# Second layer of two small networks: weight halves side by side in one 512-column matmul, the halves added by ScalarE's copy and GpSimd

## The chip, the core and the metric

The kernel runs on one core of a Trainium2 chip. Its engines are TensorE (PE; PEld is its weight load), VectorE (DVE), ScalarE (ACT), GpSimd (POOL) and the DMA queue of SyncE (SP). TensorE writes to PSUM, a small memory of accumulation banks (512 float32 columns each here); the other tiles lie in SBUF. The metric is the time of one execution in device microseconds. Before the change the median of three runs is 865.88 us (861.5 to 867.78).

## What is computed

The input is 2 x 3136 rows of 256 numbers. A Fourier filter with soft thresholds comes first, then two mixtures (small two-layer networks, each added to its input), the second behind a real two-dimensional Fourier transform:

```python
def _moe_ref(x, g_ln, w_ch1, w_ch2):
    mu = np.mean(x, axis=-1, keepdims=True)
    var = np.mean((x - mu) ** 2, axis=-1, keepdims=True)
    xn = (x - mu) / np.sqrt(var + 1e-06) * g_ln
    ch = np.maximum(xn @ w_ch1, 0.0) @ w_ch2       # 256 -> 1024 -> 256
    return (x + ch).astype(np.float32)

def _moe2_ref(x, w_ch1, w_ch2):
    mixed = np.real(np.fft.fft(np.fft.fft(x, axis=1), axis=2)).astype(np.float32)
    u = x + mixed                                  # then as above, without g_ln
    ...
    return (u + ch).astype(np.float32)
```

## The kernel before, in words

Matmuls run on operands rounded to 12 bits of mantissa (float32r). To keep float32's accuracy each operand is split into a main part and a rest (`h` and `l`), and a product is three matmuls into one PSUM tile: main x main, main x rest, rest x main (`mm3`, `mm3r`).

Rows go through the mixtures in chunks of up to four tiles of 128 rows, 13 chunks for each mixture (26), 49 tiles each. Per chunk (`Chunk`, driven by `run_mlp`): `prep` normalizes the next chunk's rows on VectorE (statistics, then four scalings into `q`), `trans` transposes them on TensorE, `l1(f)` makes one of eight blocks of 128 hidden channels for all rows of the chunk (six matmuls of up to 512 columns into a `psa` tile; ScalarE writes the main part after the relu, VectorE the rest), and `l2(i)` makes the output of one row tile (for each of the eight blocks three matmuls of 256 columns into a `psb` tile, 24 in all), after which VectorE adds the tile's input and `store` sends it out. A `psb` tile is one PSUM bank of 512 columns, of which 256 are used; there are two of them. The stationary operand of the second layer is the hidden block, the moving one the weights.

The weights come as float64, and `decode64` on VectorE splits them into main part and rest, in an SBUF tile `r3a` for the first mixture and `r2b` for the second. Each has a half of main parts and a half of rests; `w_views` names their pieces.

Between the mixtures stands a 98-point transform of each of the two batch halves (`Stage98`), 16 steps for each: load a piece of `dX`, three GpSimd instructions on it (`split`), a ScalarE copy, a subtraction on VectorE or GpSimd (the rest), three matmuls into `psc`, a ScalarE copy out, a small GpSimd copy, a store to `dA`. The first half's 16 steps hang on the chunks 7 to 10 of the first mixture, since they need all of that half's rows, the last of which chunk 6 stores; the second half's hang on chunks 0 to 3 of the second mixture, since they need the first mixture's last chunk. VectorE, ScalarE and GpSimd each take their instructions in the order of the program, which a scheduler lays out with its own estimate of times; an instruction that waits holds up all behind it on its engine.

`wk` tiles rotate over a few buffers by tag. Tag `t98` (TB = 2) has two buffers, used before the change by the inverse transform's tiles alone, which ends before the first chunk's second layer.

## Time and profile before

| | |
|---|---|
| median of three runs | 865.88 us (861.5 to 867.78) |
| the profiled execution: its own time | 860.46 us |
| its span, first to last instruction | 858.7 us |
| TensorE matmul busy | 824.3 us, 96% of the span, 5235 matmuls |
| VectorE, ScalarE, GpSimd busy | 529.8, 282.1, 129.5 us |
| granted TensorE clock | 0.986 of full speed in the mean |

The profile is that of one execution. Busy time of TensorE overlaps, since a matmul is shown until it leaves the pipeline; the distance between starts of matmuls tells what one costs. "Idle before" with an arrow names what ended an engine's wait. The chain of waits is followed back from the last instruction.

### The profile page before, as it was taken

To read this page: it belongs to the slowest core of one execution; us is meant where nothing else is said; L and a number is where in the kernel's file an instruction comes from. 1 tells how busy PE (TensorE), PEld (TensorE's weight loads), DVE (VectorE), ACT (ScalarE), POOL (GpSimd) and SP (SyncE) were. 2 spreads that over 40 slices of the span, in tenths; PEclk is the share of its full clock that TensorE was granted. 3 is DMA by queue.
4 is the path that set the end of the run, shared out by engine and by line. 5 is a ranking of instruction groups with operands and counts; after the bars stand their busy time and mean duration, and the time that the engine had idled before them with its cause. 6 is when DMAs were issued, how large, how long until landed. Compare 5 with 4: busy or idle time off the path is not lost.

```text
span 858.7 us, 13585 instructions
## 1 busy us (share of the span) xinstructions
PE 824.3 (96%) x5235; PEld 719.0 (84%) x5235; DVE 529.8 (62%) x1216; ACT 282.1 (33%) x541; POOL 129.5 (15%) x184
## 2 busy tenths in 40 slices
PE   7999999868999999998999998999999999999997
PEld 2778978824999989986989997888899899999996
DVE  5677999476456894458557356476456656445652
ACT  0222355246222222244342224334432323322321
POOL 0112321220100000069310005244120000000000
PEclk9999999969999999999999999999999999999999
DMA  8630201534110321155223104433323122210001
GB/s 229 182 101 27 74 27 49 175 123 142 59 50 18 108 78 50 63 152 155 79 96 116 61 26 115 119 97 112 117 64 88 46 65 63 74 50 22 17 21 30
DMA packets 47956, 71.66 MB, mean 83 GB/s; under 512 B 11748, under 2 KB 32236, under 8 KB 47696
## 3 DMA queue, kind: packets, MB, share of 16 engines
q1 hardware_dynamic: 47892, 70.80, 27.4%
q8 instruction: 41, 0.67, 0.3%
q14 instruction: 23, 0.19, 0.1%
HBM read 45.09 MB, written 25.69 MB: 82 GB/s over the span
## 4 chain that ended last, share of the span: by engine, by line
PE 80%; DMA 8%; DVE 6%; POOL 2%; SPq 2%; issue 1%; ACT 1%; POOLq 0%; DVEq 0%
PE psb L212 10%; PE psb L210 10%; PE psb L211 10%; PE psa L216 9%; PE psa L217 9%; PE psa L218 9%; PE psb L457 7%; PE psc L323 3%; PE psc L578 2%; PE psc L679 2%; PE psc L477 2%; DMA r<-dX 2%; PE psa L425 2%; PE psc L305 1%; DMA h<-in_x_dram 1%; DMA stg<-in_w_i_dram 1%
## 5 line engine op out<-in xcount | busy, mean ns | idle before, releaser
L602 ACT ACTIVATE h<-psa 128x512 fp32r<-128x512 f32 (+2 forms) x208 | 118.1, 572 | 264.1 <-PE psa L218 252.9
L603 DVE SCALAR_TENSOR_TENSOR h<-psa,h 128x512 fp32r<-128x512 f32 (+2 forms) x208 | 135.0, 653 | 89.6 <-ACT h L602 88.4
L212 PE MATMUL psb<-r3a,h 128*128 128x256 f32 x392 | 108.9, 284 | 2.0 <-DVE h L603 2.0
L210 PE MATMUL psb<-r2b,h 128*128 128x256 f32 x392 | 110.7, 286 | 0.0
L210 PE MATMUL psb<-r3a,h 128*128 128x256 f32 x392 | 110.1, 284 | 0.0
L211 PE MATMUL psb<-r3a,h 128*128 128x256 f32 x392 | 110.1, 283 | 0.0
L211 PE MATMUL psb<-r2b,h 128*128 128x256 f32 x392 | 109.7, 283 | 0.0
L620 DVE TENSOR_TENSOR o<-psb,yb 128x256 f32<-128x256 f32 x98 | 40.8, 421 | 110.2 <-PE psb L212 110.1
L212 PE MATMUL psb<-r2b,h 128*128 128x256 f32 x392 | 107.1, 283 | 0.0
L457 PE MATMUL psb<-wm,h 128*128 128x256 f32 (+1 forms) x600 | 86.5, 296 | 0.3 <-ACT wm L198 0.3
L216 PE MATMUL psa<-q,r2b 128*128 128x512 f32 (+2 forms) x208 | 83.0, 399 | 0.4 <-DVE h L603 0.3
L216 PE MATMUL psa<-q,r3a 128*128 128x512 f32 (+2 forms) x208 | 80.6, 387 | 2.9 <-DVE h L603 2.1
L457 PEld LDWEIGHTS psb<-wm,h 128*128 128x128 f32 (+1 forms) x600 | 75.6, 189 | 7.5 <-issue 6.2
L217 PE MATMUL psa<-q,r2b 128*128 128x512 f32 (+2 forms) x208 | 79.2, 381 | 0.0
L218 PE MATMUL psa<-q,r2b 128*128 128x512 f32 (+2 forms) x208 | 79.1, 381 | 0.0
L217 PE MATMUL psa<-q,r3a 128*128 128x512 f32 (+2 forms) x208 | 78.5, 378 | 0.0
L218 PE MATMUL psa<-q,r3a 128*128 128x512 f32 (+2 forms) x208 | 78.2, 379 | 0.0
L212 PEld LDWEIGHTS psb<-r3a,h 128*128 128x128 f32 x392 | 74.3, 191 | 2.5 <-DVE h L603 2.4
L210 PEld LDWEIGHTS psb<-r2b,h 128*128 128x128 f32 x392 | 75.0, 191 | 0.8 <-DVE o L620 0.2
L210 PEld LDWEIGHTS psb<-r3a,h 128*128 128x128 f32 x392 | 74.9, 191 | 0.8
L211 PEld LDWEIGHTS psb<-r3a,h 128*128 128x128 f32 x392 | 74.9, 191 | 0.7
L211 PEld LDWEIGHTS psb<-r2b,h 128*128 128x128 f32 x392 | 75.0, 192 | 0.4
(105 smaller groups left out, 1396.7 us busy)
## 6 DMA issues: line engine op xcount, KB each, us to landing
s<-in_moe_w_ch_dram SPq DMA_DIRECT2D x16, 512.0 KB
r<-dX SPq DMA_DIRECT2D x32, 196.0 KB
dA<-o SPq DMA_DIRECT2D x32, 196.0 KB
dY<-yg SPq DMA_DIRECT2D x12, 512.0 KB
r<-dA SPq DMA_DIRECT2D x48, 128.0 KB
yb<-dY SPq DMA_DIRECT2D x11, 512.0 KB
dX<-o SPq DMA_DIRECT2D x11, 512.0 KB
yb<-dX SPq DMA_DIRECT2D x50, 64.0 KB
```

Source lines behind the costliest of these rows:

```text
L210: nc.tensor.matmul(out=ps, lhsT=lh, rhs=rh, start=first, stop=False)
L211: nc.tensor.matmul(out=ps, lhsT=lh, rhs=rl, start=False, stop=False)
L212: nc.tensor.matmul(out=ps, lhsT=ll, rhs=rh, start=False, stop=last)
L216: nc.tensor.matmul(out=ps, lhsT=lh, rhs=rh, start=first, stop=False)
L217: nc.tensor.matmul(out=ps, lhsT=ll, rhs=rh, start=False, stop=False)
L218: ins = nc.tensor.matmul(out=ps, lhsT=lh, rhs=rl, start=False, stop=last)
L323: nc.tensor.matmul(out=ps[0:NQ, :], lhsT=cim, rhs=t, start=True, stop=True)
L425: nc.tensor.matmul(out=pa[:, 2 * u + c], lhsT=yg[b][:, k1 + u, c * 128:(c + 1) * 128], rhs=cb[:, k1 + u, :], start=True, stop=True)
L457: nc.tensor.matmul(out=ps[0:m, u * D:(u + 1) * D], lhsT=xv[:, o:o + m], rhs=wm_hl[wv][:, e, c, :], start=k == 0, stop=k == 11)
L602: nc.scalar.activation(out=h[:, 0:n], in_=ps[:, 0:n], func=AF.Relu)
L603: ins = nc.vector.scalar_tensor_tensor(out=l[:, 0:n], in0=ps[:, 0:n], scalar=0.0, in1=h[:, 0:n], op0=ALU.max, op1=ALU.subtract)
L620: nc.vector.tensor_tensor(out=self.o[:, i, :], in0=ps[:, 0:D], in1=self.y[:, i, :], op=ALU.add)
```

## The change

`w_views` and `decode64` lay the second layer's weights out so that for each hidden block the 256 main columns and the 256 rest columns are neighbours. `l2` then issues two matmuls for each hidden block in place of three: main part of the hidden block against all 512 columns, and its rest against the 256 main columns. The left half of the `psb` tile holds two of the three products' sum, the right half the third's. ScalarE copies the right half to an SBUF tile `e` (tag `t98`), VectorE adds the left half and the tile's input into `o`, and GpSimd adds `e` to `o`.

```diff
     def w_views(r):
-        return ([r[:, i, 0:2048].rearrange("p (k f) -> p k f", k=2) for i in range(2)],
-                [r[:, i, 2048:].rearrange("p (f c) -> p f c", f=NF) for i in range(2)])
+
+        v = r.rearrange("p h f -> p (h f)")
+        return ([v[:, i * 2048:(i + 1) * 2048].rearrange("p (k f) -> p k f", k=2) for i in range(2)],
+                v[:, 4096:].rearrange("p (f c) -> p f c", f=NF))
...
         def l2(self, i):
-            _, (w2h, w2l) = self.wv
+            _, w2 = self.wv
...
                 for f in range(NF):
                     h, l = self.h[f]
-                    mm3(ps[:, 0:D], h[:, ts_], l[:, ts_], w2h[:, f, :], w2l[:, f, :], f == 0, f == NF - 1)
-            nc.vector.tensor_tensor(out=self.o[:, i, :], in0=ps[:, 0:D], in1=self.y[:, i, :], op=ALU.add)
+                    nc.tensor.matmul(out=ps, lhsT=h[:, ts_], rhs=w2[:, f, :], start=f == 0, stop=False)
+                    nc.tensor.matmul(out=ps[:, 0:D], lhsT=l[:, ts_], rhs=w2[:, f, 0:D], start=False, stop=f == NF - 1)
+
+            t = wk.tile([128, 512], F32, tag="t98", name="e", bufs=TB)[:, 0:D]
+            a_copy(t, ps[:, D:2 * D])
+            o = self.o[:, i, :]
+            nc.vector.tensor_tensor(out=o, in0=ps[:, 0:D], in1=self.y[:, i, :], op=ALU.add)
+            nc.gpsimd.tensor_tensor(out=o, in0=o, in1=t, op=ALU.add)
```

In `decode64` the instructions stay eight, and only their outputs and inputs are cut in two pieces of 256 for the second layer's weights.

On TensorE, third row tile of the first chunk (`psb_1887` before, `psb_1877` in the changed kernel; `h_1739` and so on hold main part and rest of the hidden blocks, `r3a` the weights). Before:

```order
L210 MATMUL psb_1887<-r3a_182,h_1739 128x256
L211 MATMUL psb_1887<-r3a_182,h_1739 128x256
L212 MATMUL psb_1887<-r3a_182,h_1739 128x256
L210 MATMUL psb_1887<-r3a_182,h_1749 128x256
L211 MATMUL psb_1887<-r3a_182,h_1749 128x256
```

In the changed kernel, with the transposes of the next chunk that stand ahead of it and the end of the first row tile (`psb_1835`), whose bank it takes over:

```order
L630 MATMUL psb_1856<-r3a_182,h_1809 128x512
L631 MATMUL psb_1835<-r3a_182,h_1809 128x256
L631 MATMUL psb_1856<-r3a_182,h_1809 128x256
L589 MATMUL psc_1900<-ident_72,q_1829 128x128
L589 MATMUL psc_1907<-ident_72,q_1829 128x128
L589 MATMUL psc_1900<-ident_72,q_1829 128x128 x3
L589 MATMUL psc_1907<-ident_72,q_1829 128x128 x3
L630 MATMUL psb_1877<-r3a_182,h_1739 128x512
L631 MATMUL psb_1877<-r3a_182,h_1739 128x256
L630 MATMUL psb_1877<-r3a_182,h_1749 128x512
```

Two rows stand for a hidden block in place of three, and the first two row tiles end within a matmul of each other.

On VectorE, first chunk, with what an instruction waits for (an engine's name). Before:

```order
L603 SCALAR_TENSOR_TENSOR h_1809<-psa_1802,h_1809 128x512 [waits Activation_49]
L620 TENSOR_TENSOR o_1834<-psb_1835,yb_1602 128x256 [waits PE_49]
L620 TENSOR_TENSOR o_1834<-psb_1861,yb_1602 128x256 [waits PE_49]
L584 SCALAR_TENSOR_TENSOR q_1914<-psc_1915,g_sb_80,q_1913 128x512 [waits Activation_49]
L584 SCALAR_TENSOR_TENSOR q_1914<-psc_1922,g_sb_80,q_1913 128x512 [waits Activation_49]
```

In the changed kernel:

```order
L614 SCALAR_TENSOR_TENSOR h_1809<-psa_1802,h_1809 128x512 [waits Activation_49]
L636 TENSOR_TENSOR o_1834<-psb_1835,yb_1602 128x256 [waits Activation_49]
L636 TENSOR_TENSOR o_1834<-psb_1856,yb_1602 128x256 [waits Activation_49]
L595 SCALAR_TENSOR_TENSOR q_1899<-psc_1900,g_sb_80,q_1898 128x512 [waits Activation_49]
L595 SCALAR_TENSOR_TENSOR q_1899<-psc_1907,g_sb_80,q_1898 128x512 [waits Activation_49]
```

The order is the same, but the add of a row tile waits for ScalarE's copy and no longer for TensorE.

On GpSimd, where the first half's 98-point transform begins (`w` are the split pieces, `s98` the rests, `o_3312` the output of chunk 7). Before:

```order
L362 TENSOR_TENSOR w_3599<-r98_3597 98x2x127
L363 TENSOR_TENSOR w_3599<-r98_3597 98x2x127
L364 COPY w_3599<-r98_3597 98x4
L206 TENSOR_TENSOR s98_1730<-w_3409,s98_1730 98x512
L206 TENSOR_TENSOR s98_1730<-w_3519,s98_1730 98x512
```

In the changed kernel:

```order
L362 TENSOR_TENSOR w_3454<-r98_3452 98x2x127
L363 TENSOR_TENSOR w_3454<-r98_3452 98x2x127
L637 TENSOR_TENSOR o_3312<-o_3312,e_3330 128x256
L364 COPY w_3454<-r98_3452 98x4
L206 TENSOR_TENSOR s98_1730<-w_3274,s98_1730 98x512
L401 COPY o98_1731<-mid_3262 98x2
L637 TENSOR_TENSOR o_3312<-o_3312,e_3367 128x256
L206 TENSOR_TENSOR s98_1730<-w_3374,s98_1730 98x512
```

Two of the new adds (L637) stand among the splits and subtractions of the transform, ahead of the second subtraction.

## Rows read from the trace of the kernel before

**Rows 1.** Page, part 1: engine, busy us (share of the span) x instructions.
```profile
PE 824.3 (96%) x5235; PEld 719.0 (84%) x5235; DVE 529.8 (62%) x1216; ACT 282.1 (33%) x541; POOL 129.5 (15%) x184
```
**Rows 2.** Busy time by stretch: start:end, length, engines' busy us (instructions), clock, DMA.
```profile
205.00:360.00 155.00, 154.04 (x1007) 141.69 (x1006) 95.68 (x238) 42.38 (x78) 2.72 (x2) 1.00 0.23 77
360.00:412.00 52.00, 48.31 (x308) 41.36 (x307) 34.95 (x75) 22.46 (x44) 38.73 (x60) 1.00 0.47 133
...
500.00:540.00 40.00, 37.17 (x242) 33.50 (x240) 24.39 (x62) 13.34 (x29) 14.18 (x22) 0.96 0.31 83
540.00:600.00 60.00, 56.83 (x361) 50.28 (x362) 35.09 (x86) 23.94 (x49) 20.21 (x37) 1.00 0.38 109
600.00:830.00 230.00, 229.86 (x1543) 211.64 (x1542) 128.49 (x362) 73.19 (x160) 8.30 (x17) 1.00 0.20 58
```
**Rows 3.** Timeline, TensorE, second layer: start us, us, engine, line, what (33 matmuls).
```profile
508.48 0.28 PE L210 MATMUL psb<-r3a,h 128*128 128x256 f32 x1
...
512.32 0.28 PE L212 MATMUL psb<-r3a,h 128*128 128x256 f32 x1
```
**Rows 4.** Timeline, TensorE, first layer: 23 matmuls of 512 columns, 17 of 384.
```profile
329.10 0.39 PE L217 MATMUL psa<-q,r3a 128*128 128x512 f32 x1
...
334.11 0.39 PE L218 MATMUL psa<-q,r3a 128*128 128x512 f32 x1
...
348.10 0.34 PE L217 MATMUL psa<-q,r3a 128*128 128x384 f32 x1
...
350.88 0.34 PE L218 MATMUL psa<-q,r3a 128*128 128x384 f32 x1
```
**Rows 5.** Chain of waits in order of time: start us, us, what.
```profile
222.81 0.87 PE psc L578 x8
...
365.12 1.93 DMA dX<-o
...
368.08 5.11 DMA r<-dX
...
506.79 0.84 PE psc L679 x8
...
514.53 2.77 DMA dX<-o
```
**Rows 6.** Groups by line and form: busy us, mean ns, idle before with its releaser.
```profile
L602 ACT ACTIVATE h<-psa 128x512 fp32r<-128x512 f32 x176 | 104.1, 597 | 221.0 <-PE psa L218 212.0 <-PE psb L212 8.7
L620 DVE TENSOR_TENSOR o<-psb,yb 128x256 f32<-128x256 f32 x98 | 40.8, 421 | 110.2 <-PE psb L212 110.1
L362 POOL TENSOR_TENSOR w<-r 98x254 f32<-98x254 f32 x32 | 23.8, 743 | 234.6 <-DMA r<-dX 231.5 <-ACT h L602 2.0 <-DVE st L554 1.1
L198 ACT ACTIVATE w<-psc 128x256 f32<-128x256 f32 x25 | 9.5, 381 | 34.9 <-PE psc L679 34.9
L567 POOL TENSOR_SCALAR q<-yb,mv,sm 128x256 f32<-128x256 f32 x4 | 5.3, 1337 | 36.8 <-DMA dY<-yg 25.0 <-DVE sm L563 11.8
```
**Rows 7.** Timeline, VectorE, the end of the kernel.
```profile
852.46 0.42 DVE L620 TENSOR_TENSOR o<-psb,yb 128x256 f32<-128x256 f32 x1 [1.73 <-PE psb L212]
```
**Rows 8.** Timeline: when the 98-point transform starts on GpSimd, scalings, transposes that wait.
```profile
373.26 0.73 POOL L362 TENSOR_TENSOR w<-r 98x254 f32<-98x254 f32 x1 [152.89 <-DMA r<-dX]
...
365.93 1.38 DVE L567 TENSOR_SCALAR q<-yb,mv,sm 128x256 f32<-128x256 f32 x4
...
537.35 4.14 DVE L567 TENSOR_SCALAR q<-yb,mv,sm 128x256 f32<-128x256 f32 x4
...
540.27 0.33 PE L578 MATMUL psc<-ident,q 128*128 128x128 f32 x1 [0.82 <-DVE q L567]
571.46 0.44 PE L578 MATMUL psc<-ident,q 128*128 128x128 f32 x2 [0.96 <-DVE q L567]
```

More of the change, by code (lines that the diff above doesn't have):

```diff
@@ L499, in decode64, with cut @@
         v = nc.vector
+        def cut(a):
+            return a if len(dh.shape) == 2 else a.rearrange("p (f c) -> p f c", f=dh.shape[1])
         v.tensor_scalar(out=t1, in0=w, scalar1=3, scalar2=0x3FFFF000,
@@ L503, in decode64 @@
         v.tensor_scalar(out=t2, in0=w, scalar1=20, scalar2=0x7FF, op0=ALU.logical_shift_right, op1=ALU.bitwise_and)
-        v.scalar_tensor_tensor(out=dh, in0=t2, scalar=896.0, in1=t1f, op0=ALU.is_gt, op1=ALU.mult)
+        v.scalar_tensor_tensor(out=dh, in0=cut(t2), scalar=896.0, in1=cut(t1f), op0=ALU.is_gt, op1=ALU.mult)
         v.tensor_scalar(out=t2, in0=w, scalar1=0x1FF, scalar2=None, op0=ALU.bitwise_and)
         v.scalar_tensor_tensor(out=t2f, in0=low, scalar=2.0 ** -32, in1=t2, op0=ALU.mult, op1=ALU.add)
-        v.tensor_scalar(out=t1, in0=dh.bitcast(I32), scalar1=-0x800000, scalar2=None, op0=ALU.bitwise_and)
-        v.scalar_tensor_tensor(out=dl, in0=t2f, scalar=2.0 ** -20, in1=t1f, op0=ALU.mult, op1=ALU.mult)
+        v.tensor_scalar(out=cut(t1), in0=dh.bitcast(I32), scalar1=-0x800000, scalar2=None, op0=ALU.bitwise_and)
+        v.scalar_tensor_tensor(out=dl, in0=cut(t2f), scalar=2.0 ** -20, in1=cut(t1f), op0=ALU.mult, op1=ALU.mult)
     def load_mlp(w1, w2, r):
@@ L513, in f @@
             def f():
-                decode64(src, r[:, 0, o:o + 512], r[:, 1, o:o + 512])
+                if o < 2048:
+                    v = r.rearrange("p h f -> p (h f)")
+                    decode64(src, v[:, o:o + 512], v[:, 2048 + o:2048 + o + 512])
+                else:
+                    w2 = w_views(r)[1][:, (o - 2048) // D:(o - 2048) // D + 2, :]
+                    decode64(src, w2[:, :, 0:D], w2[:, :, D:2 * D])
             return f
@@ L525, in w_views @@
     def w_views(r):
-        return ([r[:, i, 0:2048].rearrange("p (k f) -> p k f", k=2) for i in range(2)],
-                [r[:, i, 2048:].rearrange("p (f c) -> p f c", f=NF) for i in range(2)])
+        v = r.rearrange("p h f -> p (h f)")
+        return ([v[:, i * 2048:(i + 1) * 2048].rearrange("p (k f) -> p k f", k=2) for i in range(2)],
+                v[:, 4096:].rearrange("p (f c) -> p f c", f=NF))
     class Chunk:
```

## The prediction

> **What bounds the kernel now.** I read the busy times first, then the busy times by stretch, the timeline where those showed gaps, and the chain of waits. TensorE is busy for 824.3 us [rows 1], and the stretches tell where it isn't. In the two long stretches of plain mixture work it lacks 155.00 - 154.04 = 0.96 us and 230.00 - 229.86 = 0.14 us [rows 2]: nothing else limits there, and VectorE, ScalarE and GpSimd have room (128, 73 and 8 of 230 us in the second). In three stretches with the 98-point transforms it lacks 3.69, 2.83 and 3.17 us, together 9.7 [rows 2]. There a chain through other engines sets the time: the last chunk's store to `dX` (1.93 us, then 5.11 us of loading, GpSimd starting at 373.26 after a wait of 152.89) [rows 5, 8], then splits, ScalarE copies and VectorE's scalings, for which the transposes wait (0.82 and 0.96 us at two of them) [rows 8]. So the change must be judged in two ways: what a second-layer step costs TensorE in the plain stretches, and what the longer way out of PSUM costs in the chained ones and at the end.
>
> **TensorE's steps.** 33 matmuls of 256 columns in the second layer start between 508.48 and 512.32: 3.84 us over 32 intervals, 0.1200 us each [rows 3]. 23 matmuls of 512 columns take 5.01 us over 22 intervals, 0.2277 each; 17 of 384 columns 2.78 us over 16, 0.1737 [rows 4]. 128 columns more cost 0.0537 and then 0.0540 us: the three lie on one line, at 2.39 columns a nanosecond (the upper clock level; granted clock 1.00 [rows 2]), and the line leaves about 0.0126 us for each matmul at no columns at all. Columns stay the same (3 x 256 = 512 + 256), one matmul of three goes, so a hidden block costs 0.2277 + 0.1200 = 0.3477 instead of 0.3600 us: 0.0123 saved. That the weight load doesn't become the bound is seen from 64-column matmuls, eight in 0.84 us, 0.105 each [rows 5]: a load needs no more than that, and it lies under a 256- or 512-column matmul of 0.120 or more. There are 98 row tiles (the add's count [rows 6]) of eight blocks, 784 in all: **9.6 us**. From both sides: nothing, if that fixed share belongs to the block and not to the matmul; 9.6 if it goes with the instruction. I take 9.6, since three sizes show the same share.
>
> The Trainium skill's page "TensorE: Matmul & The Clock Gate", section "Back-to-back issue gap", speaks against so much: isolated matmuls at the full clock come every N / 2.4 + 2.5 ns. By that a block would go from 327.5 to 325.0 ns and the change would give only 2.0 us (an estimate from that page); the 120 and 228 ns of rows 3 and 4 disagree with it, so the measured share stands.
>
> **The way out of PSUM.** ScalarE's copy: a copy of 128x256 from PSUM to SBUF takes 0.381 us [rows 6]; 98 of them are 37 us on an engine that is busy for 282 [rows 1]. VectorE's add stays at 0.421 [rows 6], but the order shows it behind the copy. GpSimd's new add of 128x256 has no row of its own: an add of 98x254 takes 0.743, a scaling of 128x256 1.337 [rows 6]. I take 0.74, the same operation, and keep 1.34 for the range; 98 of them are 73 us on an engine busy for 129. The cut outputs in `decode64` cost nothing: same counts and sizes.
>
> A bank is free again after copy and add, 0.38 + 0.42 = 0.80 us behind the last matmul, where it was 0.42. What covers this: at a chunk's change the next chunk's eight transposes stand between (0.87 us in the first chunk [rows 5]), in most chunks first-layer or projection matmuls too (projections 0.84 more [rows 5]). By the order three places have about 0.9 to 1.1 us of cover, the others more. The copies stand right behind the row tiles on ScalarE, which in the plain stretches mostly waits for TensorE (212 of its 221 us of idle time ahead of the relu [rows 6]). So nothing in the plain stretches; without cover it would be 0.4 at a chunk's change. What ScalarE's third copy waits for (two `e` buffers, so the add before last) has two row tiles' time, 5.6 us.
>
> **At the end** nothing covers it. The last add ran at 852.46 [rows 7] right behind TensorE. Now copy, add and GpSimd's add follow: +0.38 + 0.74 = **+1.1 us**.
>
> **In the chained stretches** the store to `dX` starts both chains (365.12 and 514.53 [rows 5]), so each starts +1.1 us later. In the first, two of GpSimd's adds stand ahead of the second subtraction, where GpSimd worked without pause (38.73 us of the 52 [rows 2], all of it after 373.26): +1.4 (two of 0.7 to 0.74). In the second, the first chunk's adds stand behind its subtractions, but in the next chunk the copy that frees a bank stands behind the fourth split's copy: I take +1.0 (bounds 0 and 3, four adds of 0.74). While these chains rule, the savings of the ten row tiles inside them are worth nothing: 10 x 8 x 0.0123 = +1.0.
>
> Sum: -9.6 + 1.1 + (1.1 + 1.4) + (1.1 + 1.0) + 1.0 = **-2.9 us**. The profiled execution took 860.46 us, so 857.6; the median of the runs is 0.63% above it, so 863.0 on the median's scale (-0.33%).
>
> **The rivals.**
>
> *The chains absorb the delays* (chance 0.28). The scheduler has laid out the order of all engines anew, and the chains have idle time of their own. If that is worth the 4.6 us charged above for them and the 1.0 of savings lost in them, only the end's 1.1 stays: 860.46 - 9.6 + 1.1 = 852.0, 857.3 on the median's scale (-1.0%). For it: 9.7 us of idle TensorE time is there to be won [rows 2]. Against it: GpSimd is full, and gets more.
>
> *GpSimd's adds stall the chained stretches* (0.13), the case on the other side. An add slows VectorE where both work: four scalings took 1.38 us with GpSimd idle and 4.14 with it at work [rows 8]. The page "SBUF — State Buffer", section "Who interferes with whom", of the Trainium skill says that an instruction of the one may block that of the other for its whole length; rows 8 agree in direction. An add late by that holds the `e` buffer, so ScalarE's copy, VectorE's add, the bank and TensorE. The chunks affected are those with transform steps (four of each mixture); it decides from about 1.5 us for each, and at 2 us for each of eight it is 16 us: 860.46 - 2.9 + 16 = 873.6, 879 on the median's scale (+1.5%). Against it: the adds come behind a chunk's scalings, in the order as in time.
>
> *No gain on TensorE* (0.07): a 512-column matmul followed by a 256-column one of other weights costs as much as the three. Then all but the 9.6 and the 1.0 stays: 860.46 + 5.7 = 866.2, 871.6 on the median's scale (+0.7%). Against it stand rows 3 and 4; for it, that no row has the two sizes mixed.
>
> **How the numbers follow.** My forecast has 0.52, with its own range 859 to 868 (GpSimd's add at 1.34 us would bring 0.6 at the end, at each chain's start and for each of two adds: +3.0; the first two rivals' effects in part make up the rest). The whole range reaches from the first rival, a little beyond it, to the third and into the second: 855 to 873. About 1% is what a measurement of this kernel can tell from no change, seeing that three runs spread over 0.7%. Faster by over 1%: half of the first rival and the lower edge of the forecast, 0.19; slower by over 1%: the second rival and a little of the third, 0.15; the rest 0.66.
>
> **What would show it.** Starts of second-layer matmuls 0.228 and 0.120 us apart, pairs at 0.348; the plain stretches shorter by some 0.1 us for each row tile with TensorE still full; ScalarE's copies near 0.38 and GpSimd's adds near 0.74; about 1.1 us more from the last matmul to the end. Wrong would be: pairs at 0.36 (third rival), TensorE waiting for `psb` behind VectorE in the plain stretches, or idle time in the chained stretches that is far from 9.7 + 4.6 us, on either side.

## The result, and the profile after

| | before | changed |
|---|---|---|
| median | 863.51 us (10 runs, 860.93 to 867.78) | 869.49 us (10 runs, 868.17 to 871.49) |
| profiled execution, span | 858.7 us | 867.3 us |
| TensorE busy; matmuls | 824.3 us; 5235 | 826.2 us; 4451 |
| granted clock of that execution | 0.986 | 0.975 |

The ratio is 1.0073, 95% interval 1.0052 to 1.0093: the change made the kernel slower by 0.7%, 6.3 us on a median of 863. I had forecast 0.33% less. Below, a ratio is turned into us by 863. A profile shows one execution only, and two executions of one program can differ by some us; so kernels are compared by their ratios, and profiles are read for what waits for what.

The page's first part for the changed kernel (as [rows 1]):

```profile
PE 826.2 (95%) x4451; PEld 682.2 (79%) x4451; DVE 533.5 (62%) x1216; ACT 315.7 (36%) x639; POOL 201.0 (23%) x282
```

784 matmuls fewer, and TensorE is not less busy. The same stretches as [rows 2]:

```profile
205.00:360.00 155.00, 154.04 (x812) 132.16 (x811) 96.95 (x239) 51.36 (x105) 21.38 (x27) 1.00 0.23 77
360.00:412.00 52.00, 44.91 (x225) 36.78 (x225) 35.41 (x72) 21.59 (x45) 35.90 (x59) 0.90 0.43 127
...
500.00:540.00 40.00, 35.36 (x178) 29.81 (x177) 21.52 (x64) 14.06 (x34) 9.83 (x15) 0.91 0.28 79
540.00:600.00 60.00, 56.79 (x296) 46.94 (x295) 33.33 (x76) 25.57 (x55) 25.91 (x44) 0.97 0.37 105
600.00:830.00 230.00, 229.63 (x1284) 198.70 (x1283) 131.93 (x369) 87.35 (x197) 41.40 (x63) 1.00 0.22 62
```

In the plain stretches TensorE still lacks nothing (0.96 and 0.37 us). In the three chained ones it now lacks 7.09, 4.64 and 3.21 us where it lacked 3.69, 2.83 and 3.17, and the clock in them is 0.90, 0.91 and 0.97 where it was 1.00, 0.96 and 1.00. The stretch from 412 to 500 us, without idle time before, lacks 1.68 us.

The waits of TensorE that stand for most of this (timeline, TensorE; in brackets the idle time before and what ended it), and the one of the kernel before at the last of these places:

```profile
378.65 0.71 PE L216 MATMUL psc<-s,ca_hl 98*98 98x512 f32 x1 [3.36 <-DVE mid L201]
...
397.65 0.59 PE L216 MATMUL psa<-q,r3a 128*128 128x512 f32 x1 [2.61 <-DVE h L614]
...
531.69 0.32 PE L210 MATMUL psc<-mhl,ca_hl 98*98 98x32 f32 x1 [4.49 <-DVE mhl L201]
```

```profile
522.89 0.23 PE L210 MATMUL psc<-mhl,ca_hl 98*98 98x32 f32 x1 [2.02 <-DVE mhl L201]
```

The trace tells what stood ahead of each. The first ends with `mid`, a copy on VectorE. It stands there behind the transform's subtraction, which waits for ScalarE's copy of GpSimd's split, and behind a row tile's add. ScalarE's new copy `e` had ended at 377.10, while that subtraction still ran, so it held nothing up here. All engines, from 376 us:

```profile
376.20 0.63 ACT L198 ACTIVATE s<-w 98x512 fp32r<-98x512 f32 x1 [7.67 <-POOL w L364]
...
376.73 0.37 ACT L198 ACTIVATE e<-psb 128x256 f32<-128x256 f32 x1
...
376.86 1.21 DVE L206 TENSOR_TENSOR s<-w,s 98x512 fp32r<-98x512 f32 x1 [3.15 <-ACT s L198]
...
378.00 0.41 DVE L636 TENSOR_TENSOR o<-psb,yb 128x256 f32<-128x256 f32 x1
...
378.33 0.17 DVE L201 COPY mid<-psc 98x32 f32<-98x32 f32 x1
```

In the kernel before, `mid` stands behind the same subtraction (375.50 to 376.72), and TensorE has no wait there. Between the next chunk's transposes and the transform's first step it had 24 second-layer matmuls left, where the changed kernel, which has made 30 of two row tiles' 32 matmuls ahead of the transposes, has two left. The second-layer matmuls in this stretch (us, TensorE busy with them, count, clock, DMA), before and then changed:

```profile
374.10:377.20 3.10, 3.03 (x24) 1.00 0.38 130
374.10:377.20 3.10, 0.60 (x2) 1.00 0.54 151
```

So this wait comes with where the new matmuls stand in TensorE's order, and not with the way out of PSUM.

The second wait ends when VectorE gets to the hidden blocks' rests behind four scalings that took 3.71 us. The same four (timeline, VectorE) in the changed kernel; in the kernel before; and in two kernels of below, the one with the reload ahead of a store and the one with the reload behind it:

```profile
393.28 3.71 DVE L578 TENSOR_SCALAR q<-yb,mv,sm 128x256 f32<-128x256 f32 x4
...
391.15 2.76 DVE L567 TENSOR_SCALAR q<-yb,mv,sm 128x256 f32<-128x256 f32 x4
...
392.46 5.76 DVE L573 TENSOR_SCALAR q<-yb,mv,sm 128x256 f32<-128x256 f32 x4
...
399.92 1.38 DVE L581 TENSOR_SCALAR q<-yb,mv,sm 128x256 f32<-128x256 f32 x4
```

Up to there the second and the third have the same instructions in the same order on every engine, and so have the first and the fourth. So the length of these four differs between executions of one program by more than the 3.71 and 2.76 us do, and these say nothing of the change. In the fourth, GpSimd was at work for 0.15 of the 1.38 us; in the others for 2.91, 2.76 and 5.62.

The third is the second chain's start. In the chain of waits the store to `dX` now comes from GpSimd's add and takes 6.49 us to land, where it took 2.77 [rows 5]:

```profile
365.90 3.05 DMA dX<-o
...
519.97 0.75 POOL o L637
520.74 6.49 DMA dX<-o
```

### The profile page after: what moved, and what is told of

Its sections match the earlier page's. It is cut to its first block, busy times and chain, and to the rows that moved or that the text cites. A ratio compares the mean times of both kernels' runs of the same rounds, so it can differ in the third digit from the quotient of the medians.

```text
span 867.3 us, 12231 instructions
## 1 busy us (share of the span) xinstructions
PE 826.2 (95%) x4451; PEld 682.2 (79%) x4451; DVE 533.5 (62%) x1216; ACT 315.7 (36%) x639; POOL 201.0 (23%) x282
## 4 chain that ended last, share of the span: by engine, by line
PE 78%; DMA 8%; DVE 6%; issue 2%; SPq 2%; POOL 2%; ACT 1%; POOLq 0%; DVEq 0%; ACTq 0%
PE psb L630 18%; PE psa L216 9%; PE psb L631 9%; PE psa L217 9%; PE psa L218 9%; PE psb L457 7%; PE psc L323 3%; PE psa L425 2%; PE psc L696 2%; PE psc L477 2%; PE psc L589 2%; PE psc L305 2%; DMA r<-dX 2%; DMA s<-in_moe_w_ch_dram 1%; DMA stg<-in_w_r_dram 1%
## 5 line engine op out<-in xcount | busy, mean ns | idle before, releaser
L637 POOL TENSOR_TENSOR o<-o,e 128x256 f32<-128x256 f32 x98 | 73.2, 756 | 409.4 <-DVE o L636 397.5
L630 PE MATMUL psb<-r2b,h 128*128 128x512 f32 x392 | 139.3, 403 | 0.8 <-DVE o L636 0.7
L630 PE MATMUL psb<-r3a,h 128*128 128x512 f32 x392 | 137.1, 399 | 0.7 <-DVE o L636 0.7
L631 PE MATMUL psb<-r2b,h 128*128 128x256 f32 x392 | 106.2, 282 | 0.0
L631 PE MATMUL psb<-r3a,h 128*128 128x256 f32 x392 | 104.9, 281 | 0.0
L198 ACT ACTIVATE e<-psb 128x256 f32<-128x256 f32 x98 | 35.9, 383 | 187.5 <-PE psb L631 187.2
L216 PE MATMUL psa<-q,r3a 128*128 128x512 f32 (+2 forms) x208 | 81.3, 391 | 6.2 <-DVE h L614 5.5
L630 PEld LDWEIGHTS psb<-r2b,h 128*128 128x128 f32 x392 | 72.5, 190 | 16.8 <-DVE o L636 1.7
L630 PEld LDWEIGHTS psb<-r3a,h 128*128 128x128 f32 x392 | 71.7, 189 | 16.1 <-PE psc L589 0.9
L217 PE MATMUL psa<-q,r3a 128*128 128x512 f32 (+2 forms) x208 | 79.8, 384 | 0.0
L218 PE MATMUL psa<-q,r3a 128*128 128x512 f32 (+2 forms) x208 | 78.8, 384 | 0.0
L631 PEld LDWEIGHTS psb<-r3a,h 128*128 128x128 f32 x392 | 74.2, 189 | 3.9
L631 PEld LDWEIGHTS psb<-r2b,h 128*128 128x128 f32 x392 | 74.7, 190 | 3.0
L198 ACT ACTIVATE yg<-psc 98x512 f32<-98x512 f32 (+2 forms) x58 | 47.8, 854 | 76.2 <-PE psc L477 59.0
```

Of the source, the lines that this page charges most:

```text
L198: nc.scalar.activation(out=o, in_=i, func=AF.Copy, scale=scale)
L216: nc.tensor.matmul(out=ps, lhsT=lh, rhs=rh, start=first, stop=False)
L217: nc.tensor.matmul(out=ps, lhsT=ll, rhs=rh, start=False, stop=False)
L218: ins = nc.tensor.matmul(out=ps, lhsT=lh, rhs=rl, start=False, stop=last)
L630: nc.tensor.matmul(out=ps, lhsT=h[:, ts_], rhs=w2[:, f, :], start=f == 0, stop=False)
L631: nc.tensor.matmul(out=ps[:, 0:D], lhsT=l[:, ts_], rhs=w2[:, f, 0:D], start=False, stop=f == NF - 1)
```

## Experiments: each half of the change alone

**The matmuls without the way out.** After the changed kernel:

```diff
-            t = wk.tile([128, 512], F32, tag="t98", name="e", bufs=TB)[:, 0:D]
-            a_copy(t, ps[:, D:2 * D])
...
-            nc.gpsimd.tensor_tensor(out=o, in0=o, in1=t, op=ALU.add)
```

> The changed kernel's matmuls, but the right half of the PSUM bank (h times the weights' rest) is neither copied by ScalarE nor added by GpSimd, so that product is missing from the output. In the changed kernel a pair of matmuls came every 0.3536 us, against 0.3600 for the three before: 784 x 0.0064 = 5.0 us. Theory 1 (the way out of PSUM, over ScalarE's and GpSimd's queues, opens gaps on TensorE in the chained stretches, and each gap is followed by some us at 1.2 GHz): with the way out gone the gaps of 2.6 to 4.5 us go and the granted clock is that of before, so 863.5 - 5.0 = 858.5 us, ratio 0.993 to 0.996. Rival (the two sizes of matmul cost as much as the three, and the way out is hidden): it stays with the changed kernel, 866 to 869, ratio 1.003 or more.

Measured: 1.0006 (0.9972 to 1.0040), +0.5 us. Neither of the two: the matmuls cost nothing, but the 5 us do not reach the end either. The profile is of an execution (859.0 us) near the lower end of the twelve (857.9 to 869.5). TensorE stands in the first chain here too, without any way out, where the kernel before did not:

```profile
376.86 0.68 PE L216 MATMUL psc<-s,ca_hl 98*98 98x512 f32 x1 [2.13 <-DVE mid L201]
```

**The way out without the matmuls.** In the kernel before:

```diff
-            nc.vector.tensor_tensor(out=self.o[:, i, :], in0=ps[:, 0:D], in1=self.y[:, i, :], op=ALU.add)
+            t = wk.tile([128, 512], F32, tag="t98", name="e", bufs=TB)[:, 0:D]
+            a_copy(t, ps[:, 0:D], scale=0.0)
+            o = self.o[:, i, :]
+            nc.vector.tensor_tensor(out=o, in0=ps[:, 0:D], in1=self.y[:, i, :], op=ALU.add)
+            nc.gpsimd.tensor_tensor(out=o, in0=o, in1=t, op=ALU.add)
```

> The kernel before with its three matmuls, and the longer way out alone: ScalarE copies the sum's PSUM half times zero into an extra tile, GpSimd adds that tile to the result. Theory 1: the way out costs what the changed kernel lost plus what its matmuls saved, 6.0 + 5.0 = 11 us, ratio 1.008 to 1.016, with gaps of over 2 us on TensorE in the chained stretches (360 to 600 us) and granted clocks near 0.5 behind them. Rival (the way out is hidden but for the end's 1.1 us and the two chains' 1.1 each, the loss comes from how the matmuls are ordered): 863.5 + 1.1 to 4.6 = 864.6 to 868, ratio 1.001 to 1.005.

Measured: 1.0079 (1.0050 to 1.0107), +6.8 us (4.3 to 9.2). The way out alone costs as much as the whole change. With the run before it the two halves add up to 7.3 us, against 6.3 for the change.

**ScalarE's copy alone.** The same without the last line and the scale:

> The kernel before with ScalarE's copy of each sum from PSUM into an extra tile ahead of VectorE's add, which waits for it; no add on GpSimd, and the tile is read by nothing. With the GpSimd add as well the kernel before took 1.0079 times its time. Theory a (ScalarE's queue and the longer hold of the bank do it): 868 to 870 us, ratio 1.005 to 1.008. Theory b (GpSimd's adds do it, at the stores that start the chains and at the end): 863.5 to 865.5, ratio 1.000 to 1.002.

Measured: 1.0100 (1.0067 to 1.0132), +8.6 us, above theory a's range and far from b's: over the whole kernel the copy alone costs no less than copy and add. Chain by chain the profiles say more. SyncE's timeline of this kernel, and then the chain of waits of the way out alone:

```profile
523.67 0.32 SPq L631 DMA_DIRECT2D dX<-o  x1
...
526.50 0.90 SPq L375 DMA_DIRECT2D m<-dX  x1
...
521.06 6.71 DMA dX<-o
```

From the store that starts the second chain to the end of the span it took 344.2 us here (523.67 to 867.9), as in the kernel before (514.53 [rows 5] to 858.7), and the next load could go out 2.83 us behind the store. With GpSimd's add as well it took 347.8 us (521.06 to 868.9), and the store landed after 6.71. So behind that store the copy alone lost nothing in these profiles, and GpSimd's add, with the late landing, some 3.6 us. What the copy costs must then lie ahead of that store; by which wait, no run shows. This kernel's longest wait of TensorE was 2.45 us, in the first chain, for transposes whose scalings took 6.21 us:

```profile
395.73 6.21 DVE L567 TENSOR_SCALAR q<-yb,mv,sm 128x256 f32<-128x256 f32 x4
...
402.00 0.42 PE L578 MATMUL psc<-ident,q 128*128 128x128 f32 x1 [2.45 <-DVE q L567]
```

**Both adds on VectorE**, no copy and no GpSimd:

```diff
-            t = wk.tile([128, 512], F32, tag="t98", name="e", bufs=TB)[:, 0:D]
-            a_copy(t, ps[:, D:2 * D])
...
-            nc.gpsimd.tensor_tensor(out=o, in0=o, in1=t, op=ALU.add)
+            nc.vector.tensor_tensor(out=o, in0=o, in1=ps[:, D:2 * D], op=ALU.add)
```

> The changed kernel's matmuls with both halves added by VectorE, left half plus input, then right half, both from PSUM: no copy on ScalarE, no add on GpSimd. 98 more VectorE instructions of 0.42 us, 41 us on an engine that is busy for 62 per cent. Theory 1 in the form that the queues of ScalarE and GpSimd are to blame (the copy stands behind a transform's copy that waits for GpSimd): the gaps go, and 863.5 - 5.0 + 0.4 (end) + 0.4 to 1.5 (two chains) = 859 to 861, ratio 0.995 to 0.998. Rival (any longer way out does it, whichever engine): 866 to 870, ratio 1.003 to 1.008.

Measured: 1.0126 (1.0091 to 1.0160), outside both. So it isn't ScalarE's queue as such: a second instruction on the way out of PSUM costs on VectorE too, and no less. Here, too, one add frees the input tile and a later one finishes the output, and the store that starts the second chain landed late, after 6.99 us.

## Experiments: where it is lost

A function decides which chunks have the new form; the others keep `mm3` and the single add:

```diff
+        def wide(self):
+            if self in mlp1:
+                return mlp1.index(self) not in (6, 7, 8, 9, 10, 12)
+            return mlp2.index(self) not in (0, 1, 2, 3, 4, 12)
...
```

> The changed form in the plain chunks alone (55 of 98 row tiles); the chunks around the two chained stretches (first mixture's 7th to 11th, second mixture's first five) and the last chunk of each mixture keep the three matmuls of 256 columns and the single add of the kernel before. Theory 1: the chained stretches and the clock are as before, the plain ones save 55 x 8 x 0.0064 = 2.8 us: 860.7, ratio 0.996 to 0.998, and no new gap of over 1.5 us on TensorE. Rival (the loss is spread over all row tiles): half of the changed kernel's loss remains, 866 to 867, ratio 1.003 to 1.004.

Measured: 860.59 us, 0.9963 (0.9934 to 0.9992), -3.2 us. This is what theory 1 had: in the plain chunks the change does what it is for, and its way out is free there.

**The first chain's chunks alone in the old form** (6 to 10 of the first mixture):

> The changed form everywhere but in the five chunks around the first chain (first mixture's 7th to 11th), which keep the three matmuls of 256 columns and the single add. By the milestones of the two profiles the changed kernel lost 5.4 us between the stores that start the two chains (365.90 to 520.74 against 365.12 to 514.53). Theory 2: that comes back: 864 to 865 us, ratio 1.000 to 1.002. Rival (the second chain and the end carry the loss): 867.5 to 869, ratio 1.005 to 1.007.

Measured: 1.0023 (0.9997 to 1.0049).

**The second chain's chunks and the end in the old form** (12 of the first mixture; 0 to 4 and 12 of the second):

> The changed form everywhere but in the chunks around the second chain and at the end (the last chunk of the first mixture, the first five and the last of the second). By the milestones 2.4 us plus the end's 1.1 were lost behind 520 us. Theory 2: these come back, 866 to 867.5, ratio 1.003 to 1.005. Rival (the second chain carries most): 862 to 864, ratio 0.999 to 1.001.

Measured: 1.0015 (0.9990 to 1.0040). The one is 4.3 and the other 5.0 us below the changed kernel's +6.3, and each about 5 above the -3.2 of the kernel with the plain chunks alone: the two chains (the second with the kernel's end) share the loss about evenly. That the milestones put 5.4 us on the first and 2.4 on the second didn't hold. They are read from one profile each, and the time between the two stores varies by more than that in one program: 149.4 us in the kernel before (365.12 to 514.53 [rows 5]), 155.3 in the kernel with the reload ahead of the store (363.69 to 518.96), the same instructions in the same order up to there.

## Experiments: the granted clock

After the wait of 3.36 us the clock of the changed kernel was at 0.50, the lower of the two levels (1.2 GHz), for a whole stretch, and after the one of 4.49 us again (busy time by stretch, columns as in [rows 2]):

```profile
376.00:380.00 4.00, 1.35 (x3) 1.02 (x4) 2.91 (x5) 2.96 (x6) 4.00 (x9) 0.68 0.33 101
380.00:384.00 4.00, 4.00 (x11) 3.05 (x10) 1.62 (x3) 1.63 (x3) 4.00 (x8) 0.50 0.67 205
...
528.00:532.00 4.00, 0.31 (x2) 0.34 (x3) 0.60 (x4) 0.12 (x1) 0.00 (x0) 0.88 0.68 76
532.00:536.00 4.00, 3.85 (x14) 3.16 (x13) 3.97 (x11) 2.06 (x5) 3.52 (x6) 0.50 0.58 189
```

Over its ten runs the mean clock was 0.9785, over 116 runs of the kernel before 0.984, which is 5 us of full speed. Whether that is a cause was tested by giving TensorE something to do in the gaps. First at both places (in `middle`, ahead of the second chain's first matmuls, and in `step`, ahead of the first chain's first step):

```diff
+            if self is s4[1]:
+                for _ in range(16):
+                    nc.tensor.matmul(out=ps, lhsT=r3[:, 0, 0:128], rhs=r3[:, 0, 0:512], start=True, stop=True)
...
+            if self is s4[0] and g == 0:
+                for _ in range(10):
+                    nc.tensor.matmul(out=ps, lhsT=r3[:, 0, 0:128], rhs=r3[:, 0, 0:512], start=True, stop=True)
```

> The changed kernel with 26 more matmuls of 512 columns whose result is overwritten (10 ahead of the first transform step of the first chain, where TensorE stood idle for 3.36 us, 16 around the second chain's first wait of 4.49 us); they write a PSUM tile that the next matmul starts anew, and add nothing else. Theory 2 (what the gaps cost is for a good part the granted clock, which falls to 1.2 GHz behind them: time lost to the clock 18.7 us in the changed kernel's runs against 14.0 before): with the gaps filled by some 5 us of work the clock stays up there, although no wait got shorter, and 3 to 6 us come back: 863.5 to 866.5 us, ratio 1.000 to 1.003, mean granted clock 0.983 or more. Rival (the waits alone are the cost): no gain, ratio 1.007 or above, or 1.01 if the added matmuls delay what stands behind them.

Measured: 1.0118 (1.0087 to 1.0149). A misfire at the first place: the bank that the fillers write came free only when the wait was over, so they ran behind the gap and at the lower clock.

```profile
381.31 4.14 PE L403 MATMUL psc<-r3a 128*128 128x512 f32 x10 [3.38 <-DVE mid L201]
```

So each place was tried alone, the first with a bank of `psa`, which is free there (`pf = psum("a")`, 13 matmuls):

> The changed kernel with 13 more matmuls of 512 columns (13 x 0.2277 = 3.0 us) in one place alone: in front of the first transform step of the first chain, where TensorE stood idle for 3.36 us and showed 0.68, 0.50 and 0.97 of the clock in the next three stretches of 4 us (some 3.4 us lost). They write a PSUM bank that is free there and that nothing reads. Theory 2 (the clock falls because TensorE stood idle): the idle time turns into work at no cost, the clock stays up, 3.4 us come back: 866 us, ratio 1.003 to 1.004, and no stretch under 0.95 between 376 and 388 us. Rival (the clock there has another cause, or the waits behind it take the gain back): ratio 1.007 or more.

Measured: 1.0067 (1.0042 to 1.0092), no change. This time the fillers stood in the gap, and the clock stayed at 1.00:

```profile
376.00:380.00 4.00, 3.72 (x19) 2.82 (x17) 1.61 (x4) 1.78 (x4) 3.85 (x7) 1.00 0.46 142
380.00:384.00 4.00, 3.81 (x17) 3.07 (x18) 2.41 (x5) 2.93 (x6) 4.00 (x8) 1.00 0.52 140
```

The rival is right that nothing comes back. That TensorE is not what the chain waits for, so that a faster TensorE only waits longer for the next step, would explain it; it is argued and not shown, since with the fillers the other engines' instructions also come in a somewhat different order.

> The changed kernel with 16 more matmuls of 512 columns (3.65 us) around the second chain's first wait alone, where TensorE stood idle for 4.49 us and then showed 0.88, 0.50 and 0.77 of the clock (3.4 us lost, where the kernel before lost 1.7). They write the PSUM tile that the next matmul starts anew. Theory 2: the idle time goes to about 1 us, the clock stays up, up to 3.4 us come back: 866 to 867, ratio 1.003 to 1.005, no stretch under 0.9 between 528 and 540 us. Rival: ratio 1.007 or more, since the wait is only moved to a later place.

Measured: 1.0083 (1.0055 to 1.0111), no gain either; the wait fell to 0.95 us, and the clock fell a little later. And in the kernel with the new form in the plain chunks alone, with 8 fillers in `middle()`:

> The kernel with the changed form in the plain chunks alone, and 8 more matmuls of 512 columns (1.8 us) around the second chain's first wait, where it showed 2.36 us of idle time and then 0.91 and 0.66 of the clock (1.7 us lost). Theory 2: that clock stays up, 1.7 us less: 859, ratio 0.994 to 0.995. Rival (the added work costs its 1.8 us, or the clock falls a little later): 860.5 to 862.5, ratio 0.996 to 0.999.

Measured: 0.9959 (0.9935 to 0.9983), the same as without fillers (0.9963), although the clock now stood at 1.00 in the stretches that had 0.91 and 0.66. The lower clock is real, but at no place could it be won back.

## Experiments: SyncE's queue

The order of SyncE's rows shows what the store's 6.49 us come from. Before, the last rows ahead of the second chain's first load (`m98`; a wait for DMAHW is one for an earlier transfer):

```
L540 DMA yb_1602<-dX10_68 64x256 [waits DMAHW5_49]
L628 DMA dX11_69<-o_4832 128x1024 [waits DMAHW6_49,DVE_49]
L540 DMA yb_1602<-dX10_68 128x1x256 [waits DMAHW7_49]
L375 DMA m98_5030<-dX11_69 98x32x1 [waits DMAHW6_49,DMAHW0_49]
```

In the changed kernel:

```
L551 DMA yb_1602<-dX10_68 64x256 [waits DMAHW5_49]
L551 DMA yb_1602<-dX10_68 128x1x256 [waits DMAHW6_49,DVE_49]
L645 DMA dX11_69<-o_4607 128x1024 [waits DMAHW7_49,Pool_49]
L375 DMA m98_4785<-dX11_69 98x32x1 [waits DMAHW7_49,DMAHW0_49]
```

Before, VectorE's add freed the input tile `yb` and finished the output `o` at one time. Now it frees `yb`, and GpSimd's add finishes `o` later (0.75 us in the chain above); so the reload of `yb`, 128 single rows in mirrored order, has come ahead of the store.

**The reload ahead of the store, in the kernel before** (the loads of the second mixture's chunks 2 and 3 are written in front of the store, nothing else):

```diff
...
+                    if chunks is mlp1 and k == 12 and i == ch.nt - 1:
+                        for c in mlp2[2:4]:
+                            c.load_y()
+                        for ins in mlp2[3].loaded:
+                            es.enter_context(tc.issue_after(ins))
+                    ch.store(i)
```

> The kernel before with the one reload (mirrored rows of the second mixture's fourth chunk) ahead of the store that starts the second chain, as it stands in the changed kernel; its matmuls and its way out of PSUM are untouched. Theory 3: the store's landing goes from 2.77 to some 6.5 us and the whole becomes 2.5 to 4 us longer, ratio 1.003 to 1.005. Rival (the second chain has room): ratio 0.999 to 1.001.

Measured: 1.0044 (1.0022 to 1.0065), +3.8 us: two rows of one queue swapped. Up to that store all engines have the instructions and the order of the kernel before; behind it one of TensorE's and one of VectorE's have moved by a few places. From that store to the end of the span the two profiles have 347.2 and 344.2 us. SyncE's timeline; the load behind the store has to wait for its landing, 7.04 us in the chain of waits:

```profile
509.82 9.08 SPq L541 DMA_DIRECT2D yb<-dX  x6
518.96 0.46 SPq L634 DMA_DIRECT2D dX<-o  x1
526.06 0.92 SPq L375 DMA_DIRECT2D m<-dX  x1
```

**The reloads behind the stores, in the changed kernel**, at both chains:

```diff
-                sp.dma_start(out=o if n > 1 else o[:, 0, :], in_=ap)
+                with ExitStack() as es:
+                    if late is not None and ap is self.loads[-1][3]:
+                        es.enter_context(tc.issue_after(late.stored))
+                    sp.dma_start(out=o if n > 1 else o[:, 0, :], in_=ap)
...
```

> The changed kernel with one reload of an input tile put behind the store that starts each chain (for the second: the mirrored rows of the second mixture's fourth chunk; for the first: the load of the first mixture's ninth chunk). Nothing else is changed by hand. Theory 3 (the reload ahead of the store makes the store's landing longer: 6.49 us against 2.77 at the second chain, 3.05 against 1.93 at the first, and each chain starts by so much later): both fall to near 2.8 and 1.9, and 3.7 + 1.1 = 4.8 us come back: 864.7, ratio 1.001 to 1.003. Rival (the store's landing is hidden, or something else is late next): ratio 1.006 or more.

Measured: 1.0078 (1.0052 to 1.0104), no gain. TensorE's wait at the second chain fell to 1.52 us, but the first chain, whose reload was moved too, got a wait of 4.99 us for the scalings behind the later load, and its store landed after 3.45 us and not after some 1.9: for the first chain theory 3 failed. So the second chain's pair of rows was swapped alone; the order on all other engines is then that of the changed kernel:

> The changed kernel with two neighbouring rows of SyncE's queue swapped: the reload of mirrored rows behind the store that starts the second chain, instead of ahead of it. All other engines' orders are those of the changed kernel. Theory 3 (in the kernel before the opposite swap cost 0.44 per cent, 3.8 us): 2.5 to 4 us come back: 865.5 to 867, ratio 1.003 to 1.0045. Rival (the second chain is held by something else as well, since the other kernel with this swap gained nothing): 1.006 or more.

Measured: 1.0060 (1.0037 to 1.0082). The store landed in 2.8 us and TensorE's wait fell from 4.49 to 2.03 us:

```profile
524.69 0.32 SPq L648 DMA_DIRECT2D dX<-o  x1
525.11 0.53 SPq L554 DMA_DIRECT2D yb<-dX  x1
527.51 0.90 SPq L375 DMA_DIRECT2D m<-dX  x1
```

but only 1.1 us of it (not to be told from nothing) reach the end, where the kernel before lost 3.8 by the opposite swap. In the two profiles the time from that store to the end of the span is 344.5 us against the changed kernel's 346.6. That the reload ahead makes the store land late is shown by both swaps; what it costs is shown for the kernel before, and for the changed kernel it lies between nothing and some 3.7 us. With the first chain's chunks in the old form (there both reloads were moved):

> The changed form everywhere but in the five chunks around the first chain, as in the run before (ratio 1.0023, its second store landed after 6.86 us), now with the reloads behind the stores. Theory 3: the landing goes to 2.8 us, some 4 us come back: 861 to 862, ratio 0.997 to 0.999, near the kernel with the changed form in the plain chunks alone (0.9963). Rival: no gain, ratio 1.001 to 1.003.

Measured: 1.0008 (0.9982 to 1.0034), against 1.0023 with the reload ahead; the intervals overlap.

## Experiments: the order of the two matmuls

The pair's matmuls need not alternate. With all eight of 512 columns of a row tile first, then its eight of 256:

```diff
                 for f in range(NF):
                     h, l = self.h[f]
                     nc.tensor.matmul(out=ps, lhsT=h[:, ts_], rhs=w2[:, f, :], start=f == 0, stop=False)
+                for f in range(NF):
+                    h, l = self.h[f]
                     nc.tensor.matmul(out=ps[:, 0:D], lhsT=l[:, ts_], rhs=w2[:, f, 0:D], start=False, stop=f == NF - 1)
```

First in the kernel with the new form in the plain chunks alone:

> The kernel with the changed form in the plain chunks alone, and in it the eight matmuls of 512 columns of a row tile first, then the eight of 256, instead of one and one. In the changed kernel a 512 followed by a 256 took 0.2355 to 0.236 us, a 512 followed by a 512 in the first layer 0.2305 to 0.236 (0.2277 in its fastest stretch). Theory m (the alternation of sizes costs what was missing from 9.6 us): starts 0.228 and 0.120 apart, a block 0.348 instead of 0.353, 440 x 0.005 = 2.2 us less than with one and one: 858.4, ratio 0.994. Rival (a 512 costs the 0.235 whatever stands beside it, only the fastest stretch had less): a block 0.353 to 0.356, 860 to 861, ratio 0.996 to 0.997.

Measured: 857.40 us, 0.9938 (0.9914 to 0.9962): the best version of the study, -5.4 us. Then in all chunks, with the reloads behind the stores:

> The changed form in all chunks, the eight matmuls of 512 columns of a row tile ahead of its eight of 256, and the reloads behind the stores. If the reloads' place is worth 4.8 us and the order of the matmuls 2 to 3 (as in the plain chunks, 0.9963 to 0.9938), it comes to 862, ratio 0.998 to 1.000; if ScalarE's copy still opens gaps around the first chain, as in the kernel with the first mixture's chunks changed (1.0015), 1.001 to 1.004.

Measured: 0.9970 (0.9947 to 0.9992), -2.6 us, better than either forecast: with this order and the reloads moved, the change in all chunks is a small gain. The next load went out 2.82 us behind the second chain's store. And the order alone in the changed kernel:

> The changed kernel with the eight matmuls of 512 columns of a row tile ahead of its eight of 256, and nothing else changed. The kernel with this order and both reloads moved had 0.997, the one with the reloads moved alone 1.0078. Theory p (the order of the pair matters by itself: alternating, every second matmul needs a rest from VectorE, and TensorE stands in the chained stretches): 861 to 863, ratio 0.997 to 1.000. Rival (the order only helps together with the reloads behind the stores): 866 to 868, ratio 1.003 to 1.006.

Measured: 863.23 us, 1.0002 (0.9981 to 1.0023). The order alone takes back 6.1 of the change's 6.3 us. Part of it is seen in TensorE's steps. Us for a block of one 512 and one 256 (or three 256), from the starts of all unbroken stretches of second-layer matmuls:

| | 210 to 360 us | 610 to 830 us |
|---|---|---|
| before | 0.3603 | 0.3621 |
| changed | 0.3527 | 0.3540 |
| changed, the 512s first | 0.3483 | 0.3500 |

With the 512s first, rows of the timeline are sets of eight (226.52 to 228.36, 0.230 each) or, over two row tiles, of 15 (652.16 to 655.56, 0.227 each):

```profile
226.52 2.00 PE L630 MATMUL psb<-r3a,h 128*128 128x512 f32 x8
228.36 1.12 PE L633 MATMUL psb<-r3a,h 128*128 128x256 f32 x8
...
652.16 3.56 PE L630 MATMUL psb<-r2b,h 128*128 128x512 f32 x15
655.56 0.99 PE L633 MATMUL psb<-r2b,h 128*128 128x256 f32 x7
```

Alternating costs 0.0044 and 0.0040 us a block, 784 x 0.0042 = 3.3 us. The other 2.8 us are a little more than the intervals of the two ratios leave open (2.5), and the other engines' order is not the same either. In this kernel's profile the longest waits in the first chain were 2.37 and 1.65 us, the first of them for `mid` as in the changed kernel; the second chain's store still landed late, after 6.67 us. With the reloads moved as well (0.9970, the run before) it is 2.8 us less, with intervals that overlap by a little.

## Why the prediction was wrong

**TensorE's steps: the term that failed.** The sum had 9.6 us, 0.0123 for each of 784 blocks, of which 1.0 was to be lost: -8.6. The run with the matmuls alone has +0.5, and these 9.1 us are nearly the whole distance from the forecast -2.9 to the measured +6.3. Two things were wrong with the term. First its size: a block took 0.3527 and 0.3540 us, 0.0076 and 0.0081 less than before, so 6.1 us in all. I had put a 512-column matmul at the 0.2277 of rows where one 512 follows another [rows 4], and no row had the two sizes mixed, as the third rival said. In the changed kernel's alternation, the 256 started 0.235 and 0.237 us behind the 512 in the mean of the two stretches:

```profile
223.88 0.40 PE L630 MATMUL psb<-r3a,h 128*128 128x512 f32 x1
224.12 0.28 PE L631 MATMUL psb<-r3a,h 128*128 128x256 f32 x1
224.24 0.40 PE L630 MATMUL psb<-r3a,h 128*128 128x512 f32 x1
...
228.83 0.40 PE L630 MATMUL psb<-r3a,h 128*128 128x512 f32 x1
```

That is 14 pairs in 4.95 us, 0.3536 each. In the order that I had reckoned with unawares, all 512s first, the forecast was right: 0.3483 and 0.3500, which is 0.0120 and 0.0121 less than before. (The rate in [rows 4] was read slightly wrong: 256 columns more for 0.1077 us are 2.38 columns a nanosecond and not 2.39; nothing hangs on it.) The formula of the Trainium skill (page "TensorE: Matmul & The Clock Gate", section "Back-to-back issue gap"), which speaks of isolated matmuls and would give 0.0025 us a block, was too low for either order. Second its reach: I took ten row tiles to be worth nothing. The runs say that the saving arrives from the 55 of the plain chunks alone: 440 x 0.0078 = 3.4 us, measured 3.2; with the new matmuls everywhere and no longer way out, 0.5 us were lost. By which wait the saving is lost around the chains stays open: the one for `mid` comes with the new matmuls, but the kernel with the 512s first has it too and is level with the kernel before.

**The way out: about the right sum, for the wrong reason.** I charged 1.1 at the end, 2.5 and 2.1 in the chains, 5.7 us; alone it cost 6.8 (4.3 to 9.2). Sizes were right: ScalarE's copies 0.383 us, GpSimd's adds 0.756 (I had taken 0.381 and 0.74):

```profile
L637 POOL TENSOR_TENSOR o<-o,e 128x256 f32<-128x256 f32 x98 | 73.2, 756 | 409.4 <-DVE o L636 397.5 <-DVE sm L574 8.3 <-DMA out_dram<-o 2.7
...
L636 DVE TENSOR_TENSOR o<-psb,yb 128x256 f32<-128x256 f32 x98 | 39.8, 421 | 135.4 <-ACT e L198 135.2
L198 ACT ACTIVATE e<-psb 128x256 f32<-128x256 f32 x98 | 35.9, 383 | 187.5 <-PE psb L631 187.2
```

The end was right as well: from the last matmul's start (859.37) to GpSimd's end 2.02 us, where [rows 7] give 0.74 from 852.14.

```profile
859.75 0.38 ACT L198 ACTIVATE e<-psb 128x256 f32<-128x256 f32 x1 [0.68 <-PE psb L631]
860.16 0.43 DVE L636 TENSOR_TENSOR o<-psb,yb 128x256 f32<-128x256 f32 x1 [0.63 <-ACT e L198]
...
860.67 0.72 POOL L637 TENSOR_TENSOR o<-o,e 128x256 f32<-128x256 f32 x1 [0.34 <-DVE o L636]
```

"Nothing in the plain stretches" held: TensorE stayed full there. But in the first chain I charged two of GpSimd's adds ahead of a subtraction (1.4 us), and in the second ScalarE's copy behind a split's copy (1.0), and no run shows either: over the whole kernel the copy alone cost no less than copy and add, and behind the second chain's store it lost nothing in its profile. What GpSimd's add does cost is a term that the sum hasn't: since it finishes the output after the input tile is free, the reload comes ahead of the store, and the store lands late. That is in SyncE's queue, which I hadn't looked at although the order showed it (3.8 us in the kernel before; of it some 1 us could be won back in the changed kernel). And the copy, for which the sum has 0.38 us at the first chain's start, seems to lose more than that ahead of the second chain's store.

**The rivals.** "The chains absorb the delays" is refuted: they lost more. "GpSimd's adds stall the chained stretches" named the stretches rightly, but its price of 16 us was far too high. The mechanism exists in small: in the changed kernel two scalings took 0.74 us ahead of one of GpSimd's new adds (365.03, 0.85 us) and the next two 1.15 beside it, so an add did not always come behind a chunk's scalings, and cost 0.4 us where it didn't.

```profile
363.73 0.74 DVE L578 TENSOR_SCALAR q<-yb,mv,sm 128x256 f32<-128x256 f32 x2
...
364.87 1.15 DVE L578 TENSOR_SCALAR q<-yb,mv,sm 128x256 f32<-128x256 f32 x2
```

"No gain on TensorE" gave 871.6 us, near the 869.5, because hardly any of the gain arrived, not because there was none. Of what I said would show it wrong, the idle time in the chained stretches came: 14.9 us against 9.7 + 4.6 = 14.3 is by itself no surprise, but 1.68 more lie between 412 and 500, and TensorE was slower in and behind these waits.

**What stays open.** How the way out's 6.8 us divide between the place of ScalarE's copy behind the transform's copies and the bank that is held longer: with the second add on VectorE the copy was gone and the loss was no smaller. The store's landing is part of it in the way out alone (6.71 us) and not with ScalarE's copy alone (2.83), which lost no less, by its profile ahead of that store. VectorE's scalings, which I suspected from [rows 8], explain nothing by themselves: the second set of the first chain took from 1.38 us (in a kernel with 1.0060) to 8.62 (1.0126), but 4.13 in one with 0.9970, and it varies from execution to execution of one program. Nor is it settled why the matmuls' order gives back some 3 us more than its steps.

## What to carry to other kernels

Judge a saving by the stretch in which it falls: 55 of 98 row tiles brought all that the change was worth, and leaving it out of the others turned +6.3 into -3.2 us, or -5.4 with the same-sized matmuls in a row. When a result gets a second writer on a slower engine, look at every queue in which its input's release and its output's store meet: the reload may overtake the store. And take the price of an instruction from a row that stands in the order in which it will be issued.

## What the runs showed of the hardware

- A 512-column matmul followed by one of 256 columns on other stationary data costs more than each in a row of its own size: 0.3527 to 0.3540 us a pair alternating, 0.3483 to 0.3500 in rows.
- A 512 KB store issued right behind a 128 KB load of single mirrored rows landed after 6.49 to 7.04 us in the profiles of seven kernels (the changed one, its 512s-first form, the way out alone, both adds on VectorE, the first chain in the old form, the fillers in the first gap, the reload ahead), and with that load behind it after 2.75 to 2.77 us in six (before among them).
- Four scalings of 128x256 on VectorE took 1.37 to 1.39 us in the 11 sets of the kernel before in the two plain stretches (GpSimd idle beside them), and at one place in the first chain from 1.38 us (GpSimd at work for 0.15 of it) to 8.62 (at work for 8.35). At that place two executions of the same instructions in the same order differed by 3.0 us (2.76 and 5.76).
- Keeping TensorE busy through a wait of 3.36 us kept its granted clock at 1.00 where it had fallen to 0.50, and didn't change the time.
